# A spectral filter and an MLP on one core: the roots of tiles 0 and 1 move to ScalarE, the second fifth of W1 is loaded ahead of tiles 2 and 3

## The chip, the cores and the metric

The kernel runs on one core of a Trainium2 chip. The metric is device time in microseconds (us) of one execution; less is better. A core has five engines, each with its own instruction stream: TensorE (PE in the profile; its weight loads are shown apart as PEld), VectorE (DVE), ScalarE (ACT), GpSimd (POOL) and SyncE (SP), which here only issues DMA transfers. They work at the same time and wait for each other through semaphores. Matmul results land in PSUM, eight banks of which VectorE and ScalarE empty into SBUF.

## What is computed

```python
xn = _layernorm(x, axis=-1)                      # x: 2048 x 640, bf16
return x + _A_ref(xn, A_w_r, A_w_i) + _B_ref(xn, B_w1, B_b1, B_w2, B_b2)

def _layernorm(x, axis=-1, eps=1e-5):
    m = jnp.mean(x, axis=axis, keepdims=True)
    v = jnp.var(x, axis=axis, keepdims=True)
    return (x - m) / jnp.sqrt(v + eps)

def _A_ref(x, w_r, w_i):
    X = jnp.fft.rfft2(x.astype(jnp.float32), axes=(-2, -1)) * (w_r + 1j * w_i)
    return jnp.fft.irfft2(X, s=(S, D), axes=(-2, -1)).astype(jnp.bfloat16)

def _B_ref(x, w1, b1, w2, b2):
    h = _gelu(jnp.einsum("bsd,df->bsf", x, w1) + b1)     # w1: 640 x 1536
    return jnp.einsum("bsf,fd->bsd", h, w2) + b2         # w2: 1536 x 640
```

The layer norm has no learned scale. Its result goes through a two-dimensional Fourier filter and, apart from that, through a two-layer MLP with a gelu; both are added to x.

## The kernel before

The 2048 rows stand as 16 tiles of 128 partitions by 640 columns, x0 to x15. For each tile VectorE computes statistics of the two halves of the columns (L670), joins them to mean and variance (L672, tensor `mv`), and normalizes the tile into `T` with `(x - mean) * rstd` (L695). Between the two stands the reciprocal root `rstd`: GpSimd raises the variance (the epsilon is already in it) to the power -0.5 (L674). Tile 0 is normalized in two parts, columns 0 to 255 and 256 to 639, so that its first two blocks of 128 columns can go on early; all others in one.

A normalized tile is used twice. The MLP needs it transposed, in `xnT`: tiles 0 to 3 are transposed by TensorE against an identity matrix (L714) and copied out of PSUM by ScalarE (L561) or VectorE (L562); tiles 4 to 15 by a DMA transpose that SP issues (L702). The Fourier part folds each pair of tiles on VectorE (L726, L730), and TensorE multiplies the folds by the table `gtab` as the first step of the transform along the rows.

The first MLP layer contracts 640 columns in five blocks of 128, so W1 is loaded in five transfers of 128 x 1536, the fifths `w1_0` to `w1_4`. For tiles 0 and 1 the work is laid out by blocks: for each of the twelve 128-wide pieces of the hidden layer five matmuls add up in PSUM, those of fifths 0 and 1 for each tile apart (128 columns, "single-tile"), the rest for both tiles at once (256 columns). The gelu on ScalarE (L774) empties each result into `gT`. Then come tiles 2 and 3 and the later blocks, the Fourier steps in between, and the second layer, the inverse transform and the sum with x at the end.

What sets the order is a table written out by hand, `ORDER`: for each engine the numbers of all operations, in the order in which they stand on that engine. The numbers count the operations as the program creates them. A planner goes through the table with its own costs and landing times (`LAND`, `LATE`) to choose PSUM banks and buffers, and works out which operation has to wait for which; it doesn't change the order. So an engine that waits holds everything behind it. All matmuls but the transposes are recorded on L550, a helper's line.

The loads of x, W1 and the tables all go through SP's queue: x0, x1, w1_0, x2 and x3 in one transfer, w1_1, w1_2, w1_4, w1_3, x4 and x5, x6 and x7, gtab, and so on. `load_x(c, n)` loads n tiles from tile c in one transfer. ScalarE begins with a load of the table that holds the tanh gelu (L599); plain copies need no other table. Before the first real work TensorE runs 38 matmuls on zeros.

## Time and profile before

| what | us |
|---|---|
| median of three runs (146.36 to 146.63) | 146.58 |
| the profiled execution | 146.47 |
| its span, first to last instruction | 145.2 |
| TensorE busy | 139.2 |
| VectorE busy | 112.6 |
| ScalarE busy | 81.0 |
| GpSimd busy | 24.0 |

The profile is one execution. Each row of its timeline gives the start in us from the span's start, the duration of the group, the engine, the line, the operation, what it writes and reads, how many instructions are joined in the row, and in square brackets the idle time of that engine ahead of it and who ended it. A row with SPq is the issue of a transfer. A row of the list of DMA issues gives the size and the time from issue to landing; such rows are taken here over a window that holds one issue. The stretches give each engine's busy time within from:to, with the number of instructions, the granted TensorE clock, the DMA share and GB/s. The chain of work that ended last is listed in order of time as start, duration and what ran.

### The profile page before, as it was taken

The page shows a single profiled execution, that of the slowest core. Times are in us where ns is not written, and L with a number is a line of the kernel's source. Part 1 is how long each engine was busy: PE and PEld are TensorE (multiplying, and loading weights), DVE is VectorE, ACT ScalarE, POOL GpSimd, SP SyncE. Part 2 cuts the span into 40 slices and gives each one's busy share as a digit, 9 for nine tenths or more (in the row PEclk, how much of TensorE's full clock was granted, in tenths as well). Part 3 has the DMA queues.
Part 4 walks back from the last instruction along what each step waited for, and adds up shares of the span by engine and source line. Part 5 has one row for each costly group of instructions (what it writes and reads, how often), then busy time and mean ns, then how long its engine had stood idle before and what let it go on. Part 6 is the DMA issues. An engine that isn't in the chain of part 4 may idle for free.

```text
span 145.2 us, 4067 instructions
## 1 busy us (share of the span) xinstructions
PE 139.2 (96%) x1702; PEld 90.0 (62%) x1720; DVE 112.6 (78%) x235; ACT 81.0 (56%) x145; POOL 24.0 (17%) x40
## 2 busy tenths in 40 slices
PE   7799999999999999999999999999999999999994
PEld 7589998988465454446544645554446666656573
DVE  1999999999844449889966967992432998998984
ACT  3208999999989769763555633206376755201000
POOL 2330302206100027220100220000055700000000
DMA  4999998999997827939676571453559895103225
GB/s 109 337 403 347 319 172 265 155 181 235 268 188 151 192 51 147 228 86 179 130 202 123 62 151 34 41 120 80 95 108 212 178 214 183 58 5 135 93 103 168
DMA packets 30841, 23.63 MB, mean 163 GB/s; under 512 B 20456, under 2 KB 26856, under 8 KB 30696
## 3 DMA queue, kind: packets, MB, share of 16 engines
q1 hardware_dynamic: 28432, 17.81, 51.7%
q0 software_dynamic: 2368, 5.57, 17.9%
q8 instruction: 13, 0.21, 0.6%
q14 instruction: 4, 0.03, 0.1%
q10 hardware_dynamic: 24, 0.00, 0.0%
HBM read 13.54 MB, written 2.62 MB: 111 GB/s over the span
## 4 chain that ended last, share of the span: by engine, by line
PE 91%; DVE 4%; issue 2%; DMA 2%; POOL 0%
PE ps L550 91%; DVE stats L670 2%; DMA X<-in_A_x_dram 2%; DVE T L695 1%; DVE mv L672 0%; POOL rstd L674 0%; PE ps L714 0%; DVE xnT L562 0%; DVE W L957 0%
## 5 line engine op out<-in xcount | busy, mean ns | idle before, releaser
L550 PE MATMUL ps<-xnT,W 128*128 128x256 bf16 (+2 forms) x384 | 58.7, 300 | 0.1
L550 PE MATMUL ps<-W,gT 128*128 128x512 bf16 (+3 forms) x380 | 55.7, 292 | 1.6 <-issue 1.1
L550 PEld LDWEIGHTS ps<-W,gT 128*128 128x128 bf16 x396 | 30.3, 98 | 23.5 <-issue 1.6
L550 PEld LDWEIGHTS ps<-xnT,W 128*128 128x128 bf16 x384 | 33.3, 98 | 16.2 <-issue 1.6
L774 ACT ACTIVATE gT<-ps,b1col 128x256 bf16<-128x256 f32 (+1 forms) x72 | 35.3, 557 | 6.8 <-PE ps L550 6.5
L670 DVE BATCH_NORM_STATS2 stats<-X 128x6 f32<-128x320 bf16 x32 | 13.9, 475 | 2.1 <-DMA X<-in_A_x_dram 2.1
L561 ACT ACTIVATE Wf<-ps 128x960 bf16<-128x960 f32 (+1 forms) x8 | 7.0, 901 | 13.5 <-PE ps L550 13.5
L942 POOL DMA_DIRECT2D X<-in_A_x_dram x8 | 7.1, 1012 | 39.8 <-DMA Wf<-in_A_w_r_dram 17.0
L841 DVE TENSOR_TENSOR T<-Y,Wf 128x1288 bf16<-128x1288 bf16 x16 | 12.7, 825 | 0.0
L942 POOL DMA_DIRECT2D xnT<-in_A_x_dram x8 | 7.8, 1246 | 25.1 <-ACT xnT L924 25.1
L674 POOL TENSOR_TENSOR rstd<-mv,mhalf 128x2 f32<-128x2 f32 (+1 forms) x10 | 7.1, 714 | 26.6 <-DVE mv L672 26.5
L561 ACT ACTIVATE Xb<-ps 128x960 bf16<-128x960 f32 (+1 forms) x7 | 7.7, 1104 | 6.8 <-PE ps L550 6.7
L562 DVE CAST Y<-ps 128x644 bf16<-128x644 f32 x8 | 6.5, 828 | 5.4 <-PE ps L550 5.4
L561 ACT ACTIVATE XV<-ps 128x1280 bf16<-128x1280 f32 (+3 forms) x10 | 9.5, 962 | 0.7 <-PE ps L550 0.7
L562 DVE CAST Xb<-ps 128x960 bf16<-128x960 f32 (+1 forms) x5 | 5.9, 1177 | 4.1 <-PE ps L550 4.0
L730 DVE TENSOR_TENSOR T<-T 128x512 bf16<-128x512 bf16 (+1 forms) x32 | 8.5, 312 | 0.0
L695 DVE TENSOR_SCALAR T<-X,mv,rstd 128x640 bf16<-128x640 bf16 (+2 forms) x17 | 7.1, 430 | 0.9 <-POOL rstd L674 0.6
L896 DVE TENSOR_TENSOR Wf<-Wf 128x960 bf16<-128x960 bf16 (+1 forms) x12 | 7.0, 597 | 0.5 <-ACT Wf L561 0.3
L957 DVE TENSOR_TENSOR W<-ps,X 128x640 bf16<-128x640 f32 x8 | 6.5, 820 | 1.1 <-PE ps L550 1.1
L957 DVE TENSOR_TENSOR W<-ps,xnT 128x640 bf16<-128x640 f32 (+2 forms) x10 | 6.7, 686 | 0.7 <-PE ps L550 0.7
L845 DVE TENSOR_TENSOR Z<-T 128x644 bf16<-128x644 bf16 x16 | 7.1, 487 | 0.1
L550 PE MATMUL ps<-etab,XV 32*128 32x160 bf16 (+1 forms) x128 | 7.2, 232 | 0.0
(55 smaller groups left out, 130.5 us busy)
## 6 DMA issues: line engine op xcount, KB each, us to landing
X<-in_A_x_dram POOLq DMA_DIRECT2D x8, 320.0 KB, 4.6
xnT<-in_A_x_dram POOLq DMA_DIRECT2D x8, 320.0 KB, 5.0
out_dram<-W SPq DMA_DIRECT2D x15, 160.0 KB, 1.8
X<-in_A_x_dram SPq DMA_DIRECT2D x7, 320.0 KB, 7.3
W<-in_B_w_dram SPq DMA_DIRECT2D x5, 384.0 KB, 5.8
W<-in_B_w_dram SPq DMA_DIRECT2D x4, 480.0 KB, 7.6
Wf<-in_A_w_i_dram SPq DMA_DIRECT2D x6, 160.5 KB, 6.2
Wf<-in_A_w_r_dram SPq DMA_DIRECT2D x6, 160.5 KB, 3.9
```

Of the source, the lines that this page charges most:

```text
L550: ins = e.matmul(o_, lhsT=lw, rhs=rh, start=st, stop=sp_, skip_group_check=True)
L561: return e.activation(dst(), src(), ACT.Copy, scale=scale)
L562: return e.tensor_copy(dst(), src())
L670: st_op[c] = K.op([("dve", 0.393)], pr, lambda e, _, c=c, h=h: e.bn_stats(stats[:, c, 6 * h:6 * h + 6], view(X, c * D + H2 * h, [[1, H2]]) ...
L674: K.op([("pool", 0.65)], 500, lambda e, _, a=a, b=b: e.tensor_tensor(out=rstd[:, a:b], in0=mv[:, a:b, 1], in1=mhalf[:, a:b], op=ALU.pow), ...
L695: o = K.op([("dve", 0.066 + (d1 - d0) / 1980.0)], pr, lambda e, _, c=c, n=n, xnv=xnv, d0=d0, d1=d1: e.tensor_scalar(out=xnv(n, d0, [[1, d1 ...
L730: ring_ops.append(K.op([("dve", dve_us(4 * w, 2))], pr, lambda e, _, op=op, x1v=x1v, xfv=xfv, o_=o_, o0=o0, o1=o1, w=w: e.tensor_tensor(ou ...
L774: K.op([("act", act_us(128 * nt, 1))], pr + PRIO["gelu"] + GP[bi], lambda e, _, c0=c0, nt=nt, fc=fc, hps=hps, at=at: e.activation(gT[:, fc ...
L841: filt_ops.append(K.op([("dve", dve_us(4 * KP, 2))], pr, lambda e, _, k=k, Y=Y, TB=TB, pair=pair: e.tensor_tensor(out=view(TT, TB.slot * 8 ...
L845: K.op([("dve", dve_us(2 * KP, 2))], pr, lambda e, _, TB=TB, Z=Z, r=r, op=op: e.tensor_tensor(out=view(Zb, Z.slot * 4 * KP + r * KP, [[2 * ...
L942: xo_ops[c] = K.op([("pool", 0.9)], 51 - c / 20, lambda e, _, c=c, xov=xov: e.dma_start(xov(0, D), xv[:, c, :], accum_op=ALU.add), reads=[ ...
L957: K.op([("dve", dve_us(w))], 95, lambda e, _, os_=os_, fps=fps, o0=o0, w=w, xov=xov, base=base: e.tensor_tensor(out=view(W1, OST + os_.slo ...
```

## The change

Five things change, and with them the order table.

- The reciprocal roots of tiles 0 and 1 are no longer a power on GpSimd. ScalarE takes the square root of the variance, and VectorE the reciprocal of it, in place. All other tiles keep the power.
- ScalarE so loads two tables: the one with the square root first, and the one with the gelu later.
- Tile 1 is normalized in two parts, as tile 0 was.
- x2 and x3 are loaded in two transfers, and w1_1 stands ahead of both on SP.
- The numbers of `ORDER`, `LAND` and `LATE` are new.

```diff
 ORDER = {
-    "sp": """8 13 14 17 15 16 19 18 21 22 20 27 30 23 26 28 153 155 166 168 31 32 35 46 48 37 179 181 192 194 38 39 41 34 44 33
+    "sp": """8 14 15 16 18 19 17 21 20 23 24 22 29 32 25 28 30 158 160 171 173 33 34 37 48 50 39 184 186 197 199 40 41 43 36 46
...
-LAND = {8: 3.13, 13: 3.63, 14: 5.8, 15: 8.08, 16: 9.04, 18: 11.01, 19: 10.03, 20: 14.89, 21: 11.84, 22: 12.65, 23: 17.41, 26: 18.61, 27: 15.54, 28: 19.46, 30: 16.42}
+LAND = {8: 3.12, 14: 3.6, 15: 5.85, 16: 7.0, 17: 9.3, 18: 7.4, 19: 8.0, 20: 11.2, 21: 10.3, 22: 14.89, 23: 11.84, 24: 12.65, 25: 17.41, 28: 18.61, 29: 15.54, 30: 19.46, 32: 16.42}
...
-        K.op([("act", 1.3)], 420, lambda e, _: e.preload_act_table(ACT.Gelu_apprx_tanh), writes=[Buf("table")])
+        K.op([("act", 1.3)], 420, lambda e, _: e.preload_act_table(ACT.Sqrt), writes=[Buf("table")])
+        K.op([("act", 1.3)], 420, lambda e, _: e.preload_act_table(ACT.Gelu_apprx_tanh), writes=[Buf("table2")])
...
         load_w1(2)
-        load_x(2, 2)
+        load_x(2, 1)
+        load_x(3, 1)
         load_w1(3)
...
             a, b = c0, c0 + n
+            if a < 2:
+                B_sd = Buf(f"sd{a}")
+                K.op([("act", 0.1)], 500, lambda e, _, a=a: e.activation(rstd[:, a:a + 1], mv[:, a, 1:2], ACT.Sqrt), reads=[B_mv], writes=[B_sd])
+                K.op([("dve", 0.08)], 500, lambda e, _, a=a: e.reciprocal(rstd[:, a:a + 1], rstd[:, a:a + 1]), reads=[B_sd], writes=[B_rs[a]])
+                continue
             K.op([("pool", 0.65)], 500, lambda e, _, a=a, b=b: e.tensor_tensor(out=rstd[:, a:b], in0=mv[:, a:b, 1], in1=mhalf[:, a:b], op=ALU.pow),
...
-                cuts = (0, 256, D) if not c else (0, D)
+                cuts = (0, 256, D) if c < 2 else (0, D)
...
-                    if not c + j0:
-                        tp.deps.remove(norm_ops[1])
+                    if c < 2 and not j0:
+                        tp.deps.remove(norm_ops[2 * c + 1])
...
-                    free = norm_ops[:2 * ki + 3]
+                    free = norm_ops[:2 * ki + 4]
```

The last two hunks follow from the second part of tile 1: the first two blocks of a tile don't wait for its second part, and a list of normalizations has one entry more. Behind the first 40 us or so the order on TensorE is as it was, and on SP it differs only at the head.

Where the instructions stand is shown at three places. Lines in the changed kernel are a few higher or lower (L670 is L671, L695 is L701, L714 is L720, L550 is L549). SP, at its beginning, before:

```order
L545 DMA X<-in_A_x_dram 128x640 x2
L545 DMA W1<-in_B_w1_dram 128x1536
L545 DMA X<-in_A_x_dram 128x1280
L545 DMA W1<-in_B_w1_dram 128x1536 x4
L545 DMA X<-in_A_x_dram 128x1280 x2
```

and with the change:

```order
L544 DMA X<-in_A_x_dram 128x640 x2
L544 DMA W1<-in_B_w1_dram 128x1536 x2
L544 DMA X<-in_A_x_dram 128x640 x2
L544 DMA W1<-in_B_w1_dram 128x1536 x3
L544 DMA X<-in_A_x_dram 128x1280 x2
```

The second fifth has moved ahead of tiles 2 and 3, which are now two issues; the three other fifths follow as before, one issue later.

VectorE from the first statistics on (X is the loaded x, T the normalized tile and its folds, xnT the transposed tile), before:

```order
L670 BN_STATS stats<-X 128x6 x2
L672 BN_AGGR mv<-stats 128x2
L670 BN_STATS stats<-X 128x6 x2
L672 BN_AGGR mv<-stats 128x2
L695 TENSOR_SCALAR T<-X,mv,rstd 128x256
L695 TENSOR_SCALAR T<-X,mv,rstd 128x384
L695 TENSOR_SCALAR T<-X,mv,rstd 128x640
L562 COPY xnT<-ps 128x384
L670 BN_STATS stats<-X 128x6 x2
L562 COPY xnT<-ps 128x384
```

and with the change:

```order
L671 BN_STATS stats<-X 128x6 x3
L673 BN_AGGR mv<-stats 128x2
L671 BN_STATS stats<-X 128x6
L678 RECIPROCAL rstd<-rstd 128x1
L673 BN_AGGR mv<-stats 128x2
L701 TENSOR_SCALAR T<-X,mv,rstd 128x256
L701 TENSOR_SCALAR T<-X,mv,rstd 128x384
L678 RECIPROCAL rstd<-rstd 128x1
L701 TENSOR_SCALAR T<-X,mv,rstd 128x256
L701 TENSOR_SCALAR T<-X,mv,rstd 128x384
L732 TENSOR_TENSOR T<-T 128x2x320 x2
L561 COPY xnT<-ps 128x384 x2
```

Tile 0's mean and variance stand behind the first half of tile 1's statistics, each reciprocal behind the work that follows, and tile 0's and 1's folds ahead of the copies; the statistics of tiles 2 and 3 come behind both copies. Further down, tile 3's copy out of PSUM, which ScalarE had, stands on VectorE behind the first statistics of tile 4.

TensorE from the first transposes on (ident is the identity matrix, the 128x128 rows with W1 are the single-tile matmuls, the 128x256 rows those of both tiles; a wait on d_ is one for a transfer), before:

```order
L714 MATMUL ps<-ident,T 128x128 x3
L550 MATMUL ps<-xnT,W1 128x128 x2
L550 MATMUL ps<-xnT,W1 128x128 [waits s_act]
L550 MATMUL ps<-xnT,W1 128x128 x9
L550 MATMUL ps<-xnT,W1 128x128 [waits d_15]
L550 MATMUL ps<-xnT,W1 128x128 x17
L550 MATMUL ps<-xnT,W1 128x256 [waits d_16,s_dve]
L550 MATMUL ps<-xnT,W1 128x256 x7
L550 MATMUL ps<-xnT,W1 128x256 [waits d_19]
```

and with the change:

```order
L720 MATMUL ps<-ident,T 128x128 [waits s_dve]
L720 MATMUL ps<-ident,T 128x128 x2
L549 MATMUL ps<-xnT,W1 128x128 [waits d_16,s_act]
L549 MATMUL ps<-xnT,W1 128x128 x15
L549 MATMUL ps<-xnT,W1 128x128 [waits s_dve]
L549 MATMUL ps<-xnT,W1 128x128 x23
L549 MATMUL ps<-xnT,W1 128x256 [waits d_17,s_dve]
L549 MATMUL ps<-xnT,W1 128x256 x9
L549 MATMUL ps<-xnT,W1 128x256 [waits d_21]
```

d_15 before and d_16 with the change are the second fifth, d_16 before and d_17 now the third, d_19 before and d_21 now the fifth one. All 48 single-tile matmuls now stand ahead of the third fifth, where 40 stood, and ten two-tile matmuls behind it ahead of the next one, where eight stood. The two transposes of tile 1's first part stand ahead of the first W1 matmul, and the other three of tile 0 behind it.

21 lines of the change are left out of this document (10 added, 11 removed), and 36 rows, old and new, of the table ORDER.

## The prediction

> **What bounds the kernel now.** I read the page's totals first, then the busy time by stretches, the chain that ended last, and the timeline of the first 13 us.
>
> ```profile
> span 145.2 us, 4067 instructions
> PE 139.2 (96%) x1702; PEld 90.0 (62%) x1720; DVE 112.6 (78%) x235; ACT 81.0 (56%) x145; POOL 24.0 (17%) x40
> core 0: us, PE busy (x) PEld busy (x) DVE busy (x) ACT busy (x) POOL busy (x), PEclk, DMA share, GB/s
> 5.50:12.00 6.50, 6.35 (x83) 5.40 (x84) 6.24 (x20) 1.76 (x5) 1.66 (x4) 1.00 1.02 397
> 12.00:25.00 13.00, 13.00 (x139) 11.84 (x137) 12.75 (x42) 12.88 (x31) 2.12 (x3) 1.00 1.04 262
> 12.03 38.28 PE ps L550 x391
> 143.17 0.33 DVE W L957
> ```
>
> TensorE is busy 139.2 of 145.2 us, at the full granted clock (1.00). On the chain, one piece of TensorE work runs 38.28 us unbroken from 12.03, and after that only its own issue gaps part it, to 143.17. So a microsecond is to be had only before 12 us, and what is won there arrives at the end only if nobody holds TensorE later. The row from 12 to 25 us is the warning: there VectorE (12.75 of 13.00) and ScalarE (12.88) are as full as TensorE.
>
> Where TensorE waits early is seen in its weight loads, which run just ahead of the matmuls:
>
> ```profile
> 5.50 0.11 PEld L714 LDWEIGHTS ps<-ident,T 128*128 128x128 bf16 x2 [1.08 <-DVE T L695]
> 6.26 0.22 PEld L550 LDWEIGHTS ps<-xnT,W 128*128 128x128 bf16 x4 [0.27 <-ACT xnT L561]
> 7.07 1.75 PEld L550 LDWEIGHTS ps<-xnT,W 128*128 128x128 bf16 x30
> 9.03 1.02 PEld L550 LDWEIGHTS ps<-xnT,W 128*128 128x128 bf16 x10 [0.20 <-DVE T L695]
> 10.91 0.55 PEld L550 LDWEIGHTS ps<-xnT,W 128*128 128x128 bf16 x6 [0.15 <-DMA W<-in_B_w_dram]
> W<-in_B_w_dram SPq DMA_DIRECT2D x1, 384.0 KB, 5.8
> W<-in_B_w_dram SPq DMA_DIRECT2D x1, 384.0 KB, 6.3
> W<-in_B_w_dram SPq DMA_DIRECT2D x1, 384.0 KB, 6.8
> 2.67 1.93 SPq L545 DMA_DIRECT2D W<-in_B_w_dram  x4
> ```
>
> Real work starts at 5.50. The three waits after it are 0.27 (copy of tile 0's transpose), 0.20 and 0.15, together 0.62 us. The 0.20 is put down to a normalization that these matmuls don't read; they read the third fifth of W1. The four issues from 2.67 are 0.48 apart, so the third fifth, issued at 3.15, landed 5.8 later, at 8.95: that is the real releaser. The fifths issued at 3.63 and 4.11 landed at 9.9 and 10.9. Before 9.03 TensorE had run out of work on the first two fifths that its order allowed.
>
> **The roots.** Each of tiles 0 and 1 loses a POOL power and gains a ScalarE root and a VectorE reciprocal.
>
> ```profile
> 3.10 0.89 DVE L670 BATCH_NORM_STATS2 stats<-X 128x6 f32<-128x320 bf16 x2 [2.10 <-DMA X<-in_A_x_dram]
> 4.03 0.22 DVE L672 BATCH_NORM_AGGREGATE mv<-stats 128x2 f32<-128x15 f32 x1
> 4.17 0.82 DVE L670 BATCH_NORM_STATS2 stats<-X 128x6 f32<-128x320 bf16 x2
> 5.16 0.57 DVE L695 TENSOR_SCALAR T<-X,mv,rstd 128x256 bf16<-128x256 bf16 x2
> 5.92 0.45 DVE L695 TENSOR_SCALAR T<-X,mv,rstd 128x640 bf16<-128x640 bf16 x1 [0.19 <-POOL rstd L674]
> 4.33 0.58 POOL L674 TENSOR_TENSOR rstd<-mv,mhalf 128x1 f32<-128x1 f32 x1 [2.78 <-DVE mv L672]
> 1.45 1.28 ACT L599 ACT_TABLE_LOAD   x1 [1.45 <-PEq L985]
> 6.11 0.17 ACT L656 ACTIVATE b1col<-ps 128x12 f32<-128x12 f32 x1
> 10.64 0.70 ACT L561 ACTIVATE xnT<-ps 128x640 bf16<-128x640 bf16 x1 [3.44 <-PE ps L714]
> ```
>
> Tile 0's power ended at 4.33 + 0.58 = 4.91, yet its normalization started at 5.16, because VectorE was still at tile 1's statistics: POOL cost nothing there. The new chain has the same cover. The sum of tile 0 moves behind one piece of tile 1's statistics, to about 4.3, and ends at 4.5. No root or reciprocal stands in this trace. Below, the nearest small ACTIVATE is the 128x12 copy, 0.17; above, the power itself, 0.58. I take 0.17 for the root, since one element a row is nearest to twelve. A reciprocal I take at 0.14, the distance at which the next instruction followed the aggregate (4.03 to 4.17); bounds 0.1 to 0.3. So the root is there at 4.7, the reciprocal goes at 4.8 when VectorE comes free, and tile 0's first part starts at 5.1 to 5.2: 0.0, bounds -0.1 and +0.3. Tile 1 did wait for POOL, 0.19. It now starts near 5.75, and its first part (half of the 0.57 of two parts) ends at 6.05 where the whole ended at 6.37. TensorE's two transposes of it then fit into the 0.27 wait. But before, tile 0's other three stood there before 6.26, so the first W1 matmul still starts near 6.2 with one transpose more to do (0.06), which the 0.06 earlier start pays: 0.0.
>
> The second table load, 1.28 as the first, comes behind the copy of tile 1, about 6.8 to 8.1. The cover is the idle 3.44 that ScalarE had before 10.64; without it every gelu would start 1.28 later. Cost 0.0.
>
> **The second fifth first.** It goes to SP ahead of tiles 2 and 3.
>
> ```profile
> 1.73 0.43 SPq L545 DMA_DIRECT2D W<-in_B_w_dram  x1
> W<-in_B_w_dram SPq DMA_DIRECT2D x1, 384.0 KB, 4.1
> X<-in_A_x_dram SPq DMA_DIRECT2D x1, 320.0 KB, 4.4
> 2.20 0.43 SPq L545 DMA_DIRECT2D X<-in_A_x_dram  x1
> 0.81 0.88 SPq L545 DMA_DIRECT2D X<-in_A_x_dram  x2
> X<-in_A_x_dram SPq DMA_DIRECT2D x1, 160.0 KB, 2.3
> W<-in_B_w_dram SPq DMA_DIRECT2D x1, 384.0 KB, 4.9
> ```
>
> The first fifth landed at 1.73 + 4.1 = 5.83, tiles 2 and 3 at 2.20 + 4.4 = 6.6, the second at 2.67 + 4.9 = 7.57, and a fifth takes about 1.0 (8.95 to 9.9 to 10.9). So the second now lands near 6.8, in time for the point at which TensorE has used up the first (6.2 and eight matmuls and six transposes, 0.8: about 7.0). TensorE can then do all 48 single-tile matmuls ahead of the third fifth instead of 40. At 1.75/30 = 0.058 each (the row from 7.07), 8 more are 0.47: it reaches the third fifth at 8.82 + 0.47 = 9.29 instead of 8.82. The third fifth has the same bytes ahead of it as before, and one transfer more. Tiles 0 and 1, 160 KB each and issued 0.47 apart, both landed 2.3 after their issue, so two halves take at most 0.94 where the whole took 0.77: the third lands at 8.95 to 9.12. The wait of 0.20 goes. A two-tile matmul takes 0.10 to 0.11 (1.02 for ten in the row from 9.03, its last one cut short). Ten of them bring TensorE to 10.4 (next fifth needed, there at 9.9 to 10.1), six more and five transposes (0.66 + 0.29) to 11.3 (last fifth needed, there at 10.9 to 11.1). The wait of 0.15 goes too. Term: -0.35, bounds 0.0 and -0.40. SP has one issue more, 0.47, ahead of x4, gtab and the later loads; those queue behind 4 us of transfers, so it costs them the 0.0 to 0.17 of the split alone.
>
> The Trainium skill, "DMA: Bandwidth & Descriptors", section Bandwidth, speaks against the split: it asks for transfers of 1 MiB and gives 0.95 us for 64 KB and 6.15 us for 1 MB, an estimated 0.6 us fixed for each. By that the third fifth would land at 9.5 and the term be about -0.1 instead of -0.35. The 0.47 between tiles 0 and 1 contradicts 0.6 plus their bytes, so I keep the row.
>
> **What is late next.** Tiles 2 and 3 arrive about 0.6 to 1.0 later, and VectorE does more: two reciprocals, a part more (0.57 - 0.45 = 0.12), tile 0's folds ahead of its copies, and tile 3's copy, which was ScalarE's.
>
> ```profile
> 9.06 0.83 DVE L726 TENSOR_TENSOR T<-T 128x640 bf16<-128x640 bf16 x2
> 7.43 0.34 DVE L562 COPY xnT<-ps 128x384 bf16<-128x384 bf16 x1
> X<-in_A_x_dram SPq DMA_DIRECT2D x1, 320.0 KB, 7.1
> 4.64 1.14 SPq L545 DMA_DIRECT2D X<-in_A_x_dram  x2
> 16.05 0.43 DVE L695 TENSOR_SCALAR T<-X,mv,rstd 128x640 bf16<-128x640 bf16 x1
> 15.37 5.33 SPq L702 DMA_TRANSPOSE xnT<-T  x4
> xnT<-T SPq DMA_TRANSPOSE x1, 4.5
> 22.39 3.78 PE L550 MATMUL ps<-xnT,W 128*128 128x256 bf16 x33
> ```
>
> Tile 0's folds (0.83) now stand ahead of the copies of tiles 0 and 1, which so end near 7.5 and 7.8; the first matmul that reads one is the 25th single-tile one, sixteen behind the 7.0 above, at 7.9: 0.0, with 0.1 as bound. Tile 3's copy frees ScalarE of 0.70 in the full stretch and costs VectorE some 0.5 (0.34 for 384 columns). It stands behind tile 4's first statistics (tile 4 lands at 4.64 + 7.1 = 11.74, now up to 11.9), so ends near 12.8; TensorE wants it at 12.9. Cost 0.0, bounds 0.0 and 0.3. Further on, tile 5 was normalized at 16.05 and its transpose, the second of the four SP issues (from about 16.7), landed 4.5 later at 21.2; TensorE read it from 22.39, 1.2 later. If VectorE runs 0.8 late there (0.12 + 0.28 + 0.5, less some idle), it lands at 22.0, and TensorE, 0.35 earlier, wants it at 22.04. I take 0.05 for small waits in this stretch, bounds 0.0 and 0.6.
>
> Sum: 0.0 + 0.0 - 0.35 + 0.05 = -0.30. The profiled run took 146.47 (span 145.2 and 1.27 around it), so 146.17 against its own time; the median of the runs shown is 146.58, 0.11 above it, which gives 146.28.
>
> **Rivals.** (a) Won early, given back in the full stretch. ScalarE and VectorE have 0.12 and 0.25 us free of 13, and TensorE can't be ahead of their results. For it speaks that row, against it that ScalarE loses 0.70. With 0.3 given back: 146.6.
> (b) Slower by VectorE. If it is 1.5 late at tile 5, the transpose lands at 22.7 and TensorE stands 0.66 at its first matmuls on tiles 4 and 5; with the 0.35 won that is +0.31, or 146.9. The sign turns at 1.2 late. For it: 6.24 of 6.50 busy before and more work now; against it: I can count only 0.9.
> (c) The roots cost more. At 0.58 for a root, as the power, and 0.3 for a reciprocal, tile 0 starts some 0.3 late and tile 1 with it, which takes back what the fifths won: 146.6. Slower only if they start over 0.64 late, for which no row speaks.
> (d) The second fifth doesn't come earlier, because it was not the queue that held it. It lands at 7.5, TensorE waits 0.5 at 7.0: 0.5 - 0.35 = 0.15 slower, 146.7; with tiles 2 and 3 late as well, 146.9.
> (e) The split holds the queue up by a fixed time for each transfer. The wait for the third fifth returns from 0.34 on (9.29 - 8.95); at 0.6 it is 0.26, and 0.35 - 0.26 leaves 146.5. Against it stands the 0.47 between tiles 0 and 1. This is the rule of the skill that is named above.
>
> **Numbers.** A measurement of this kernel tells about 0.2% (0.29 us) from no change. Forecast (the early waits go and the later engines follow; 145.95 to 146.45): 0.50, of it 0.36 below 146.29 and 0.14 within. (a) 0.19: 0.03 faster, 0.13 within, 0.03 slower. (b) 0.16, slower. (c) 0.06: 0.04 within, 0.02 slower. (d) 0.05: 0.01 within, 0.04 slower. (e) 0.04, within. Faster 0.39, same 0.36, slower 0.25. The range takes in (a) to (e) and most of the far bounds of the terms: 145.8 to 147.1.
>
> **What would show it.** Right: no wait in the weight loads before the first double matmuls and before the last fifth; the second fifth landing before 7.0; both roots under 0.25 and the second table load inside ScalarE's idle time; TensorE unbroken from about 11.3. Wrong: a wait of TensorE on tile 3's copy near 12.9, or on the transpose of tile 5 near 22 (b), or on gelus between 13 and 35 (a); a first transpose past 5.6 (c); a wait on the second fifth near 7 (d).

## The result, and the profile after

The changed kernel takes 148.49 us (median, 148.44 to 148.67) against 146.61 for the kernel before beside it: 1.0122 times as long, 95% interval 1.0091 to 1.0153. The forecast was 146.28, in a range of 145.8 to 147.1. Sign and range are both wrong. Ratios are taken over the executions that the chip's slower state left alone, so a ratio need not be the quotient of the two medians.

The profiled execution took 148.67, with a span of 147.1. So 1.57 us lie around the span, where 1.27 lay before: of the 2.20 between the two profiled executions, 1.9 are in the span and 0.3 outside it. The page, first the span and the busy times, then two of its costliest groups:

```profile
span 147.1 us, 4092 instructions
PE 141.6 (96%) x1720; PEld 90.1 (61%) x1720; DVE 113.3 (77%) x239; ACT 82.2 (56%) x147; POOL 23.0 (16%) x38
L549 PE MATMUL ps<-xnT,W 128*128 128x256 bf16 (+2 forms) x384 | 59.2, 300 | 1.5 <-DVE xnT L561 1.3
L671 DVE BATCH_NORM_STATS2 stats<-X 128x6 f32<-128x320 bf16 x32 | 14.0, 476 | 3.6 <-DMA X<-in_A_x_dram 3.6
```

TensorE's first-layer matmuls now have a wait of 1.3 for a copy that VectorE makes (`xnT`), and VectorE's statistics wait for loads of x. The same two stretches as before:

```profile
5.50:12.00 6.50, 6.08 (x85) 5.39 (x86) 5.93 (x21) 2.57 (x5) 1.61 (x2) 1.00 0.99 356
12.00:25.00 13.00, 11.70 (x124) 10.20 (x123) 11.53 (x36) 11.45 (x28) 1.45 (x2) 1.00 0.83 222
```

From 12 to 25 us TensorE, VectorE and ScalarE were all full; now all three have lost 1.2 to 1.4 of the 13 at the same time. The chain that ended last names where:

```profile
5.05 8.68 DMA X<-in_A_x_dram
13.73 0.02 issue
13.76 0.49 DVE stats L671
14.25 0.40 DVE xnT L561
14.65 0.05 issue
14.70 11.83 PE ps L549 x121
26.53 0.08 issue
26.61 118.39 PE ps L549 x1462
145.00 0.02 issue
145.03 0.32 DVE W L963
```

The load of tile 4, issued at 5.05, takes 8.68; VectorE's first statistics of it wait for that, tile 3's copy stands behind them, and TensorE behind the copy. Before, the chain had TensorE unbroken from 12.03, and VectorE's last instruction at 143.17. The timeline shows the parts of the change one by one:

```profile
4.60 0.20 ACT L677 ACTIVATE rstd<-mv 128x1 f32<-128x1 f32 x1 [1.85 <-DVE mv L673]
4.83 0.16 DVE L678 RECIPROCAL rstd<-rstd 128x1 f32<-128x1 f32 x1
5.43 0.11 PEld L720 LDWEIGHTS ps<-ident,T 128*128 128x128 bf16 x2 [0.66 <-DVE T L701]
6.90 1.28 ACT L599 ACT_TABLE_LOAD   x1
7.03 2.27 PEld L549 LDWEIGHTS ps<-xnT,W 128*128 128x128 bf16 x40
9.52 1.44 PEld L549 LDWEIGHTS ps<-xnT,W 128*128 128x128 bf16 x14 [0.21 <-issue]
11.84 0.28 PEld L720 LDWEIGHTS ps<-ident,T 128*128 128x128 bf16 x5 [0.17 <-DVE T L701]
13.76 0.49 DVE L671 BATCH_NORM_STATS2 stats<-X 128x6 f32<-128x320 bf16 x1 [1.44 <-DMA X<-in_A_x_dram]
14.16 0.47 DVE L561 COPY xnT<-ps 128x640 bf16<-128x640 bf16 x1
14.69 1.31 PEld L549 LDWEIGHTS ps<-xnT,W 128*128 128x128 bf16 x13 [1.58 <-DVE xnT L561]
```

And the issues of the second fifth (2.20), the third (3.62) and tile 4 (5.05), each from a window of its own; the last number is the time to landing:

```profile
W<-in_B_w_dram SPq DMA_DIRECT2D x1, 384.0 KB, 4.4
W<-in_B_w_dram SPq DMA_DIRECT2D x1, 384.0 KB, 5.8
X<-in_A_x_dram SPq DMA_DIRECT2D x1, 320.0 KB, 8.7
```

So the second fifth landed at 6.6, the third at 9.4 (8.95 before), tile 4 at 13.7 (11.7 before). A transfer is spread over sixteen DMA engines. The packets in the trace show that fifteen parts of tile 4 landed between 11.30 and 12.15, and one at 13.73. In the same stretch the trace has one packet of a queue that no load uses. The queues from 11 to 12 us:

```profile
q1 hardware_dynamic: 169, 0.41, 101.6%
q8 instruction: 1, 0.02, 6.2%
```

6.2% of sixteen engines for 1 us is one engine for all of it. The packet has 16,384 bytes, began at 11.65 and took 0.99. There are 13 of them over the execution (12.78 was the first before). The first question was whether this packet, the split or the copy's place made the loss.

### The profile page after: what moved, and what is told of

Its sections match the earlier page's. It is cut to its first block, busy times and chain, and to the rows that moved or that the text cites. A ratio compares the mean times of both kernels' runs of the same rounds, so it can differ in the third digit from the quotient of the medians.

```text
span 147.1 us, 4092 instructions
## 1 busy us (share of the span) xinstructions
PE 141.6 (96%) x1720; PEld 90.1 (61%) x1720; DVE 113.3 (77%) x239; ACT 82.2 (56%) x147; POOL 23.0 (16%) x38
## 4 chain that ended last, share of the span: by engine, by line
PE 89%; DMA 6%; SPq 3%; DVE 1%; issue 0%
PE ps L549 89%; DMA X<-in_A_x_dram 6%; SPq L544 3%; DVE stats L671 0%; DVE xnT L561 0%; DVE W L963 0%
## 5 line engine op out<-in xcount | busy, mean ns | idle before, releaser
L549 PE MATMUL ps<-xnT,W 128*128 128x256 bf16 (+2 forms) x384 | 59.2, 300 | 1.5 <-DVE xnT L561 1.3
L549 PE MATMUL ps<-W,gT 128*128 128x512 bf16 (+3 forms) x396 | 58.7, 295 | 0.0
L549 PEld LDWEIGHTS ps<-W,gT 128*128 128x128 bf16 x396 | 30.3, 98 | 23.5 <-issue 1.6
L549 PEld LDWEIGHTS ps<-xnT,W 128*128 128x128 bf16 x384 | 33.1, 98 | 17.3 <-issue 1.8
L671 DVE BATCH_NORM_STATS2 stats<-X 128x6 f32<-128x320 bf16 x32 | 14.0, 476 | 3.6 <-DMA X<-in_A_x_dram 3.6
L680 POOL TENSOR_TENSOR rstd<-mv,mhalf 128x2 f32<-128x2 f32 (+1 forms) x8 | 6.2, 779 | 29.1 <-DVE mv L673 29.1
L701 DVE TENSOR_SCALAR T<-X,mv,rstd 128x640 bf16<-128x640 bf16 (+2 forms) x18 | 7.1, 410 | 1.1 <-POOL rstd L680 1.1
L732 DVE TENSOR_TENSOR T<-T 128x640 bf16<-128x640 bf16 x16 | 7.3, 474 | 0.1
```

Of the source, the lines that this page charges most:

```text
L549: ins = e.matmul(o_, lhsT=lw, rhs=rh, start=st, stop=sp_, skip_group_check=True)
L671: st_op[c] = K.op([("dve", 0.393)], pr, lambda e, _, c=c, h=h: e.bn_stats(stats[:, c, 6 * h:6 * h + 6], view(X, c * D + H2 * h, [[1, H2]]) ...
L701: o = K.op([("dve", 0.066 + (d1 - d0) / 1980.0)], pr, lambda e, _, c=c, n=n, xnv=xnv, d0=d0, d1=d1: e.tensor_scalar(out=xnv(n, d0, [[1, d1 ...
L732: K.op([("dve", dve_us(640, 2))], pr, lambda e, _, k=k, op=op, xnv=xnv, x1v=x1v: e.tensor_tensor(out=x1v(H2 * k, [[D, 2], [1, H2]]), in0=x ...
```

## The experiments

All ratios are to the kernel before, run beside each on the same chip, with 95% intervals; 0.1% is 0.15 us. The changed kernel stands at 1.0122 (1.0091 to 1.0153) in four executions and at 1.0074 (1.0029 to 1.0118) in ten later ones. The interval of every variant of it below overlaps both, so no variant's time by itself shows that something came back. Orders are shown as diffs of the operations on one engine; "the order of before" and "the later order" are those of the kernel before and of the changed kernel.

### Does the split cost a fixed time?

The kernel before with x2 and x3 in two transfers:

```diff
-        load_x(2, 2)
+        load_x(2, 1)
+        load_x(3, 1)
```

> The kernel before with x2 and x3 in two transfers where the one stood; the second fifth stays behind them. Theory (one transfer more costs the queue 0.5 to 0.6, as the changed kernel with one transfer for both showed: third fifth at 8.78 against 9.41): second fifth at 8.0 to 8.2 instead of 7.54, third at 9.4 to 9.5 instead of 8.92, tile 4 near 12.2, or near 13.5 if the instruction packet of 12.8 still meets it; TensorE waits about 0.4 for the second and 0.5 or more for the third fifth, of which the later order gives some back: 0.3 to 0.6 % over before. Rival (the split costs 0.0 to 0.17 as forecast, and the later third fifth came from the order or the second table load): third at 8.9 to 9.1, time within 0.1 % of before.

Measured: 1.0041 (1.0021 to 1.0062); ten executions between 147.04 and 147.83. In its profile the two halves landed only 0.42 apart (6.33 and 6.75). The second fifth landed at 9.2, later than expected because a few single packets took up to 1.16, the third at 10.2, and TensorE waited:

```profile
9.25 2.07 PEld L553 LDWEIGHTS ps<-xnT,W 128*128 128x128 bf16 x28 [1.03 <-DMA W<-in_B_w_dram]
```

The time, 0.6 us over before and clear of the noise, puts the rival (0.0 to 0.17 for the split) out. This wait does not show why: two profiles with one transfer for both tiles have the like when single packets are slow (0.89 with both tables loaded, 0.62 with the unused reciprocals). The converse, the changed kernel with one transfer for both:

```diff
-        load_x(2, 1)
-        load_x(3, 1)
+        load_x(2, 2)
```

> The changed kernel with x2 and x3 in one transfer again, behind the second fifth. Theory (the split costs about 0.46, the distance at which the third fifth landed later than before, 9.41 against 8.92): the third fifth lands at 8.9 to 9.0, TensorE's wait of 0.21 for it goes; tile 4's first fifteen sixteenths land at 11.7, and the last one near 13.5, since the instruction packet still meets it; time 148.0 to 148.3. Rival 1 (the loads are slower at 6 to 8 us for another reason, the second table load or the order of rows): the third fifth still lands at 9.3 to 9.4, time 148.4 to 148.6. Rival 2 (0.4 earlier is enough for tile 4 to pass the packet): tile 4 at 11.8, time 146.8 to 147.2.

Measured: the third fifth, now issued at 3.15, landed 5.6 later, at 8.8, so the split had cost it 0.6 in this pair of profiles (9.4 against 8.8). Over all profiles the third fifth landed at a median of 9.5 in nine with the split and 8.9 in eleven without, each with a scatter of up to 0.7. The time, 1.0111 (1.0074 to 1.0148), doesn't show it, for another reason:

```profile
6.33 0.64 PEld L553 LDWEIGHTS ps<-xnT,W 128*128 128x128 bf16 x6
7.78 4.66 PEld L553 LDWEIGHTS ps<-xnT,W 128*128 128x128 bf16 x54
```

The six weight loads that took 0.37 in the changed kernel (6.25 there) take 0.64. TensorE ran at half pace up to 9.8, so it came 1.5 late to tile 2's transposes, and the instruction packet with it (12.89): tile 4 landed at 11.6, the packet met gtab. Nothing about the full loss follows from this run.

The kernel before with the second fifth ahead of the unsplit tiles 2 and 3:

```diff
 SP
+DMA w1_1
 DMA x2, x3
-DMA w1_1
```

> The kernel before with one move on SP: the second fifth of W1 ahead of x2 and x3, which stay one transfer; no other engine's order is touched. Theory 1 (the third fifth and tiles 2 and 3 set the early stretch, not the second fifth): the second fifth lands at 6.6 to 6.9, tiles 2 and 3 at 7.5 to 8.0, the third fifth as before near 8.9, so TensorE's wait for it stays at 0.2; tile 2's transposes (10.06 before) come 0.0 to 0.4 later since its normalization is later: 0.0 to 0.3 % over before. Theory 2 (as forecast, the second fifth held TensorE up): 0.1 to 0.2 % below before.

Measured: 1.0028 (0.9995 to 1.0060), six of ten executions at 146.4 to 146.9, others up to 148.2. No gain, as theory 1 had it. But its profile is not the one that theory 1 foretold: the second fifth landed at 7.9, not at 6.6 to 6.9, and tiles 2 and 3 only at 8.7. VectorE stood for them, and TensorE for a copy of tile 1 that VectorE makes behind their statistics:

```profile
8.74 0.89 DVE L673 BATCH_NORM_STATS2 stats<-X 128x6 f32<-128x320 bf16 x2 [2.10 <-DMA X<-in_A_x_dram]
9.93 0.99 PEld L553 LDWEIGHTS ps<-xnT,W 128*128 128x128 bf16 x10 [0.95 <-DVE xnT L565]
```

So this run tells what the move costs in the order of before, not what an early second fifth is worth.

### Do the roots cost anything?

The kernel before with the roots alone:

```diff
-  preload(gelu)
+  preload(Sqrt) ... preload(gelu) behind tile 1's copy
-  POOL  rstd = var ** -0.5                  (tiles 0, 1)
+  ACT   rstd = sqrt(var);  DVE  rstd = 1 / rstd
```

> The kernel before with only the roots changed: square root on ScalarE, reciprocal on VectorE for tiles 0 and 1, the square root's table first and the gelu's behind tile 1's copy; tile 1 still in one part. Theory (the 0.33 outside the span comes with the root or the reciprocal themselves, since loading both tables without using the root left it at 1.27, and the span is not touched): 1.57 to 1.66 between span and time, span as before within 0.15, time 0.2 % over before. Rival (the 0.33 comes with the changed order): 1.27, time within 0.1 % of before.

Measured: 1.0070 (1.0047 to 1.0094), 1.61 to 1.67 between span and time, but also a TensorE wait of 1.02 at 15.36 for a gelu. The planner, given the roots' own costs, had chosen other PSUM banks behind them. Told costs that keep every bank, the same change gives:

```diff
-  planner's cost of root, reciprocal: 0.1, 0.08
+  planner's cost of root, reciprocal: 0.5, 0.05
```

> The kernel before with only the roots changed as in the run of the roots alone, but with the planner told costs that leave all PSUM banks as before. Theory (the roots cost nothing inside the span; the 1.0 wait for a gelu near 15.4 came from the other banks): no wait near 15, span as before within 0.15, 1.57 to 1.66 between span and time: 0.1 to 0.35 % over before. Rival (ScalarE's second table load or the reciprocals delay the work at 12 to 16 us): a wait of 0.5 or more there again, 0.5 to 0.8 % over before.

Measured: 0.9990 (0.9958 to 1.0023), spans 145.0 to 146.1, and 1.59 to 1.67 outside. Its page and the end of its chain:

```profile
span 145.2 us, 4088 instructions
...
143.16 0.32 DVE W L966
```

VectorE's last instruction starts at 143.16, against 143.17 before: the roots and the second table load cost nothing inside the span. The 0.33 outside is theirs, and three runs look for it. Both tables, no root:

```diff
-  preload(gelu)
+  preload(Sqrt) ... preload(gelu) behind tile 1's copy
```

> The kernel before with only ScalarE's table loads changed: the square root's table first, the gelu's behind the copy of tile 1; nobody uses the root. What it is to settle: the runs of the changed kernel lie 1.57 to 1.66 above their spans, those of the kernel before 1.27 to 1.3, so 0.33 of the loss lies outside the span. Theory A (that 0.33 belongs to ending on, or starting with, another table set): time 0.3 above before, at an unchanged span. Theory B (it belongs to something else, for instance the number or order of instructions): time as before within 0.15. If the second table load also slows the loads at 7 to 8 us, the third fifth of W1 lands at 9.2 or later instead of 8.9, and the span grows by 0.2 to 0.4; if it doesn't, the third fifth stays at 8.9 to 9.0.

Measured: 1.0011 (0.9984 to 1.0038); 1.22 to 1.31 outside. Both tables again, and two square roots that nobody reads:

```diff
+  ACT   spare = sqrt(var)                   (tiles 0, 1; unused)
```

> The kernel before with both tables loaded and two square roots on ScalarE whose results nobody reads; the powers on GpSimd stay, there is no reciprocal. If the use of the square root brings the time outside the span: 1.57 to 1.66 between span and time, 146.9 to 147.2. If it is the reciprocal: 1.22 to 1.31, 146.6 to 146.9.

Measured: 0.9981 (0.9940 to 1.0022); 1.22 to 1.31. Two reciprocals that nobody reads:

```diff
+  DVE   spare = 1 / rstd                    (tiles 0, 1; unused)
```

> The kernel before with two reciprocals of a 128x1 column added on VectorE behind tile 0's and tile 1's normalization; nobody reads their results, and the powers on GpSimd and the one table load stay. If VectorE's reciprocal brings the time outside the span: 1.57 to 1.67 between span and time. If it came with the missing powers on GpSimd: 1.22 to 1.31. Inside the span 0.0 to 0.3 more, since VectorE has 0.3 more to do.

Measured: 0.9993 (0.9965 to 1.0020); 1.22 to 1.31. So neither tables nor root nor reciprocal brings it alone. What is common to all runs with 1.56 to 1.69 is that GpSimd lacks two powers; that, or root and reciprocal together, is left, and wasn't separated. (The run with 58 warm-up matmuls, below, scatters from 1.27 to 2.19 outside the span, and it has the powers.) The changed kernel with the powers back:

```diff
-  ACT   rstd = sqrt(var);  DVE  rstd = 1 / rstd
+  POOL  rstd = var ** -0.5                  (tiles 0, 1; one table)
```

> The changed kernel with the roots of tiles 0 and 1 as powers on GpSimd again and one table load, all else as changed (tile 1 still in two parts). Theory (the roots neither win nor lose inside the span; the loss there is the late tile 4 and the copy behind it): the first transposes start at 5.4 to 5.5, tile 4 lands at 13.5 to 13.8, TensorE waits 1.3 to 1.6 near 13.4, span within 0.2 of the changed kernel's 147.1; the 0.33 outside the span goes if it belongs to the tables: 1.0 % over before. Rival (the roots or the second table load are what costs): the third fifth lands below 9.0 and tile 4 below 12.5, time within 0.3 % of before.

Measured: 1.0063 (1.0030 to 1.0096), 1.22 to 1.32 outside. Inside the span it was not as expected: tile 4 landed at 12.3, and tile 6 was the late one (14.1), with a VectorE wait of 0.9 for it.

### The copy of tile 3

The kernel before with only that copy moved:

```diff
 ACT
 gelu
-copy xnT3
 DVE
 statistics of x4, first half
+copy xnT3
```

> The kernel before with one move: tile 3's copy out of PSUM goes from ScalarE to VectorE, behind tile 4's first statistics, as in the changed kernel. As forecast (tile 4 lands at 11.7, the copy ends near 12.7, just when TensorE wants it): 0.0 to 0.3 us over before, no wait of over 0.3 near 13. Theory now (the place is only as good as tile 4's landing, which was on time before because the instruction packet came at 12.8, behind it; and VectorE has no time to give): a TensorE wait of 0.0 to 0.3 near 13 and some 0.3 to 0.5 given up between 16 and 27 us: 0.1 to 0.4 % over before. A wait of over 1 near 13 would say that the copy's place alone does it, without the packet.

Measured: 1.0041 (1.0020 to 1.0062). Tile 4 landed on time (11.7), and yet the copy started at 12.94, because VectorE came to tile 4 only at 12.54:

```profile
12.54 0.49 DVE L672 BATCH_NORM_STATS2 stats<-X 128x6 f32<-128x320 bf16 x1
12.94 0.48 DVE L564 COPY xnT<-ps 128x640 bf16<-128x640 bf16 x1
```

```profile
13.60 1.98 PEld L552 LDWEIGHTS ps<-xnT,W 128*128 128x128 bf16 x19 [0.62 <-DVE xnT L564]
```

The place alone costs 0.62 here, without a late load. In the changed kernel, the copy ahead of the statistics:

```diff
 DVE
+copy xnT3
 statistics of x4, first half
-copy xnT3
```

> The changed kernel with one move on VectorE: tile 3's copy out of PSUM stands ahead of tile 4's first statistics. Theory (the loss is TensorE's wait of 1.3 to 1.6 for that copy, which VectorE holds behind tile 4's late landing): the copy runs at 12.3 to 12.8, TensorE meets no wait near 13.4, and 1.3 to 1.5 come back: 147.0 to 147.2, though tile 4 still lands at 13.7. Rival 1 (tile 4 is late for everything that reads it, and the full stretch from 12 to 25 us takes the gain back): 148.1 to 148.5. Rival 2 (the loss lies in the later order, where the offset grows by another 0.3 to 0.5 up to 44 us): the wait near 13 goes, and the time falls by less than 1.0.

Measured: 1.0065 (1.0032 to 1.0098). The wait at 13 is gone, and the time stayed above the 147.0 to 147.2 of the theory (median 147.91). TensorE waited 0.87 for the second fifth at 7 us, the sign of rival (d): it landed at 7.8 here. VectorE still waits for a load, now of tile 6 (which landed at 14.7):

```profile
12.89 0.49 DVE L565 COPY xnT<-ps 128x640 bf16<-128x640 bf16 x1
13.30 0.48 DVE L675 BATCH_NORM_STATS2 stats<-X 128x6 f32<-128x320 bf16 x1
14.76 0.49 DVE L675 BATCH_NORM_STATS2 stats<-X 128x6 f32<-128x320 bf16 x1 [0.97 <-DMA X<-in_A_x_dram]
```

And the copy back on ScalarE:

```diff
 DVE
-copy xnT3
 ACT
 gelu
+copy xnT3
```

> The changed kernel with tile 3's copy back on ScalarE, where the kernel before had it (behind the first gelu); all else as changed. Theory (the copy is what ties TensorE to tile 4's landing, and VectorE is too full to take it): TensorE has no wait of over 0.3 near 13 even if tile 4 lands at 13.7, VectorE starts tile 4's other statistics 0.47 earlier, and the time falls by 1.0 to 1.4 against the changed kernel: 0.2 to 0.5 % over before, of which 0.2 is outside the span. Rival (tile 4's own lateness costs the same a little later, at the first Fourier steps near 20 us or at the gelus near 26 us): 0.8 to 1.2 % over before.

Measured: 1.0098 (1.0062 to 1.0133), the time of the rival. No wait at 13 but 0.21, tile 4 at 12.2, tile 6 at 14.0; VectorE waited 1.26 for tile 6, and TensorE in small pieces that the profile puts to gelus:

```profile
14.00 1.28 DVE L675 BATCH_NORM_STATS2 stats<-X 128x6 f32<-128x320 bf16 x3 [1.26 <-DMA X<-in_A_x_dram]
```

```profile
PEld ps L553 <- ACT gT L784: 1.3, 4, 0.5
```

(The second fence is the first row of a list of who TensorE's weight loads waited for from 12 to 44 us: total, times, longest. Before, that list has one row, 0.3, for VectorE. What the two larger of these four waits were is read below, at the second profile of the changed kernel.)

### The instruction packet

The changed kernel with fewer, wider warm-up matmuls:

```diff
-WARM = (38, 0)          # 38 matmuls of 128 columns
+WARM = (10, 0)          # 10 matmuls of 512 columns
```

> The changed kernel with the warm-up on zeros written as 10 matmuls of 512 columns instead of 38 of 128 (the same work in time, 28 matmuls and 28 weight loads fewer). Theory (one DMA engine was held by a 16 KB packet of the instruction queue at 11.65, 0.99 long, when TensorE had issued a certain number of instructions, and so one sixteenth of tile 4 came 1.6 behind the other fifteen): with 56 instructions fewer the packet comes some 28 matmuls later, near 14.5; tile 4 lands at 12.2, the copy of tile 3 ends near 13.2, and the time is 147.0 to 147.4; gtab or x6 carries the delay instead. Rival (tile 4 is late through the queue: split, row sizes or the table load): tile 4 lands at 13.7 as before, and the time stays at 148.3 to 148.6.

Measured, in the profile: the packet at 14.13, tile 4 at 12.25, tile 6 at 13.07, and neither VectorE nor TensorE with a wait there:

```profile
12.28 0.49 DVE L675 BATCH_NORM_STATS2 stats<-X 128x6 f32<-128x320 bf16 x1
12.69 0.47 DVE L565 COPY xnT<-ps 128x640 bf16<-128x640 bf16 x1
13.10 1.67 DVE L675 BATCH_NORM_STATS2 stats<-X 128x6 f32<-128x320 bf16 x4
...
61.36 0.82 DVE L958 TENSOR_TENSOR X<-ps,X 128x640 f32<-128x640 f32 x1 [1.46 <-PE ps L553]
```

The packet follows TensorE's instructions, and with it gone from there tile 4 was on time. But the time did not fall: 1.0113 (1.0068 to 1.0157). The last row shows one place where that profile lost again: VectorE waits 1.46 for a tile that is loaded a second time there, and TensorE about 1.0 behind it. I took it for the work of a later packet, which began at 57.9 and took 1.83: fifteen parts of that reload landed by 59.5, one at 61.3. The unused reciprocals, in the order of before, bear this out. They have the same wait (1.50 at 61.35) with a packet at 58.7, fifteen parts by 59.4 and one at 61.3. So this loss belongs to no order: it depends on what a packet meets. Moved by 44 instructions instead of 56:

```diff
-WARM = (38, 0)          # 38 matmuls of 128 columns
+WARM = (16, 0)          # 16 matmuls of 306 columns
```

> The changed kernel with the warm-up on zeros as 16 matmuls of 306 columns instead of 38 of 128, 44 instructions fewer. Theory (the first instruction packet comes some 2 later, 13.3 to 13.8, behind tiles 4 and 6; VectorE has no wait of over 0.3 between 12.5 and 16.5, TensorE none of over 0.5 between 12 and 27; what stays is 0.33 outside the span and 0.4 to 0.8 of waits at 25 to 36 us of the later order): 0.4 to 0.8 % over before, against 1.2 % of the changed kernel. Rival (the waits come back elsewhere in full): 1.0 % or more over before, with a wait of TensorE of over 0.7 that is not at a reload of x.

Measured: 1.0063 (1.0031 to 1.0096), as expected in time; 1.57 to 1.69 outside the span. The packet came at 14.7, later than the 13.3 to 13.8 expected, behind tiles 4 and 6. TensorE was at half pace to 10.0 in this profile, so it came to the same instruction later, and it lost another 1.0 at the reload near 62. The other way round, the kernel before with more instructions ahead:

```diff
-WARM = (38, 0)          # 38 matmuls of 128 columns
+WARM = (58, 0)          # 58 matmuls of 80 columns
```

> The kernel before with the warm-up written as 58 matmuls of 80 columns instead of 38 of 128, so with 40 instructions more ahead of the real work. Theory (the packet of the instruction queue follows TensorE's count of instructions): it comes 20 matmuls earlier, near 10.7 instead of 12.78, and one sixteenth of tiles 4 and 5 or of the last fifth of W1 lands about 1 later (tile 4 at 12.5 to 13.2 instead of 11.7), gtab about 1 earlier relative to it. Tile 3's copy is ScalarE's there and waits for no load, so TensorE has no wait of over 0.3 near 13 if the last fifth is not the one that is met: 146.5 to 147.0; if the last fifth is met, up to 147.8. Rival (the packet's time is chance, or set by something else): the packet near 12.8, tile 4 at 11.7, time 146.4 to 146.7.

Measured: the packet came at 10.94, and tile 6 landed at 13.47 instead of 12.54, tile 4 on time: so it was tile 6 that it met. The time, 1.0040 (0.9998 to 1.0083), scatters from 146.5 to 149.5 and decides nothing.

The changed kernel once more:

> The changed kernel once more, unchanged. Theory (the instruction packet comes at 11.4 to 12.2 in every execution and holds up one sixteenth of tile 4 or of tile 6, whichever of the two it meets): one of the two lands 1.0 to 1.6 late, at 13.5 to 14.8, VectorE idles 0.9 to 1.5 between 12.5 and 16.5, and the times lie between 147.9 and 148.9. Rival (the profile of the changed kernel was an odd one out): both land by 13.2, VectorE without a wait there, and most times below 147.6.

Measured: median 148.42 of ten (147.13 to 149.35) beside 146.72; ratio 1.0074 (1.0029 to 1.0118). The packet came at 11.52 and met tile 6 (issued at 5.9, 13.6 instead of 13.1), not tile 4, and VectorE waited only 0.41. TensorE lost its time later. VectorE's row, and the first row of the list from 12 to 44 us:

```profile
13.64 1.67 DVE L671 BATCH_NORM_STATS2 stats<-X 128x6 f32<-128x320 bf16 x4 [0.41 <-DMA X<-in_A_x_dram]
```

```profile
PEld ps L549 <- ACT gT L780: 1.1, 3, 0.7
```

The list names ScalarE's gelus. But the profile infers who released a wait, and the two larger of these three ended with something else, a transpose made by DMA. (From tile 4 on the normalized tiles are turned by DMA, one transfer for each, issued by SP.) The larger wait, and the issue of tile 7's transpose at 21.20:

```profile
25.68 0.35 PEld L549 LDWEIGHTS ps<-xnT,W 128*128 128x128 bf16 x4 [0.75 <-ACT gT L780]
```

```profile
xnT<-T SPq DMA_TRANSPOSE x1, 4.4
```

This matmul is the first that reads tiles 6 and 7. The gelu that had to free its PSUM bank ended at 24.94; tile 7's transpose landed at 25.62, and TensorE went on 0.06 later. The wait of 0.21 at 34.82 ended 0.06 after tile 11's transpose landed (34.76). Together they come to the 1.0 by which this span (146.2) exceeds that of before (145.2).

All waits of over 0.2 between 23 and 36 us that the profiles of the later order put to gelus end so, 0.05 to 0.06 after the landing of tile 5's, 7's or 11's transpose. The 0.33 at 26.58 in the first profile is one of them.

The next instruction packet has a part in it. It came at 23.42 here, between the landings of tiles 6 and 7. In ten of the twenty profiles it began while the transposes of tiles 4 to 7 were under way. Tile 7's then took 3.8 to 4.5 from issue to landing, against 2.7 to 3.1 in the other ten. In the first profile it began at 24.25: fifteen parts of tile 7's transpose landed by 24.80, one at 26.52. No run moves this packet alone.

So the 1.5 at 14 us of the first profile is one form of the loss, not all of it.

### Is it the waits, or is there too much in the order?

VectorE made tolerant of both loads:

```diff
 DVE
 fold of x2, x3, first half
+copy xnT3
+fold of x2, x3, second half
 statistics of x4, first half
-copy xnT3
-statistics of x6, first half
 statistics of x5, x5, x4
+statistics of x6, first half
```

> The changed kernel with VectorE's order alone rearranged at one place: behind the first fold of tiles 2 and 3 come tile 3's copy and the second fold, which read no late transfer, and only then tile 4's statistics; tile 6's first statistics stand behind tiles 4 and 5's, not in second place. Theory (VectorE's wait for tile 4 or 6 is the loss): VectorE's idle time between 12.5 and 16.5 falls from 1.44 to 0.0 to 0.5, TensorE's waits between 12 and 27 add up to less than 0.6 instead of 1.8, and 0.9 to 1.4 come back: 0.3 to 0.7 % over before. Rival (VectorE simply has too much to do): idle time falls, but TensorE waits as much in all between 16 and 36 us, 0.9 to 1.3 % over before.

Measured: 1.0126 (1.0045 to 1.0208) in four executions, the time of the rival. VectorE had no wait for a load from 12.5 to 16.5, and TensorE lost its time later:

```profile
23.62 2.42 PEld L553 LDWEIGHTS ps<-xnT,W 128*128 128x128 bf16 x23 [1.14 <-ACT gT L784]
```

Again it isn't the gelu, which had ended at 21.95. This is the first matmul on tiles 4 and 5. Fifteen parts of tile 5's transpose landed by 21.29, one at 23.56, and the second packet began at 21.84. So the rival's reason, that VectorE has too much to do, is not shown. Nor is the order alone changed: the planner gave 60 of 135 PSUM buffers other banks, and a wait of 1.49 for a gelu at 52.62 is 0.31 in the changed kernel.

At last, three parts of the change taken back together:

```diff
-  ACT   rstd = sqrt(var);  DVE  rstd = 1 / rstd
+  POOL  rstd = var ** -0.5                  (tiles 0, 1; one table)
-  load_x(2, 1); load_x(3, 1)
+  load_x(2, 2)
 DVE
+copy xnT3
 statistics of x4, first half
-copy xnT3
```

> The changed kernel with three of its parts taken back: roots on GpSimd with one table load, x2 and x3 in one transfer (behind the second fifth), and tile 3's copy ahead of tile 4's statistics. What is left is the second fifth ahead of tiles 2 and 3, tile 1 in two parts and the later order. Theory (those three carry the whole loss: 0.33 outside the span, the copy's wait 1.3 to 1.5, the split 0.2): third fifth at 8.8 to 9.0, no wait of TensorE of over 0.2 between 7 and 20 us, 1.27 around the span, time 0.1 to 0.4 below before. Rival 1 (the later order on VectorE and ScalarE from 20 to 44 us loses 0.4 by itself): 0.1 to 0.4 above before. Rival 2 (TensorE, earlier, meets another late transfer, since the instruction packet only falls on the next one): a new wait of 0.5 to 1.0, 0.3 to 0.6 % above before.

Measured: 1.0060 (1.0023 to 1.0097), or 0.9 us. That is more than the 0.1 to 0.4 of rival 1. It is the size of rival 2, with a new wait of 0.5, but the packet is not what did it: it met gtab. 1.24 to 1.31 lie outside the span, and VectorE waits for no load. The two largest rows of TensorE's waits from 12 to 44 us:

```profile
PEld ps L716 <- DVE T L697: 0.5, 1, 0.5
PEld ps L552 <- ACT gT L776: 0.4, 2, 0.3
```

The 0.5 is tile 3's normalization, late since tiles 2 and 3 landed at 8.0. Of the 0.4, 0.26 ended with tile 11's transpose (landed 34.35). Neither row stands in the list of before. The two, 0.8, are what this span (146.0) has over that of before. No run here is faster than the kernel before by more than the intervals.

## Why the prediction was wrong

**What bounds the kernel** held: the early waits were the only place to win, and the row from 12 to 25 us was the warning. It was weighed too lightly (rivals (a) and (b), 0.19 and 0.16).

**The roots** held inside the span (0.0 forecast; 145.2 with the roots alone, 145.2 before). Root 0.20 (0.17 forecast), reciprocal 0.16 (0.14), first transposes at 5.43. The 0.33 outside the span was in no term: my sum moved only the span and took what lies around it as fixed.

**The second table load** held: 6.90 to 8.18, inside ScalarE's idle time.

**The second fifth first** failed by its size: -0.35 forecast, about -0.1 measured. The fifth landed at 6.6 (6.8 forecast), and TensorE did its 48 single-tile matmuls ahead of the third. But the third landed at 9.4, not at 8.95 to 9.12, so the wait of 0.20 stayed at 0.21; the last fifth's 0.15 went, and a wait of 0.17 for tile 3's normalization (11.84) came. Counted over all matmuls up to 12.5 us, TensorE had lost 0.1 less than before. The mis-sized term is the split, 0.0 to 0.17 forecast, 0.6 measured (9.4 against 8.8, and 0.6 of time in the order of before). I had taken the distance of two transfers at the head of an empty queue (0.47) as its price. The Trainium skill, "DMA: Bandwidth & Descriptors", section Bandwidth, was nearer: the estimate of 0.6 fixed for a transfer, worked out from that page, agrees with these runs in size, and its -0.1 for the term too. That the 0.6 is a fixed time for each transfer is not shown: in the run of the split alone the two halves landed 0.42 apart, and slow single packets had a part in the delay. Rival (e) had this part right, with a chance of 0.04.

**What is late next** is the step that failed in sign: tile 3's copy, forecast at 0.0 with bounds 0.0 and 0.3. By its place alone it costs 0.62, and in the changed kernel's first profile 1.58 of weight-load wait. Two errors are in it. VectorE reaches tile 4's statistics by its own work only at 12.2 to 12.5, so a copy behind them ends at 13.1 to 13.4, not at 12.8. And tile 4's landing was taken from one row, 11.74, with the split's delay of at most 0.17 added; it was 13.73, since that row held only as long as nothing else fell on one of the sixteen engines. That tile 4 was met is chance in part: it happened in one of the ten profiles with the later order, and in the changed kernel's other profile tile 4 landed at 12.3 and tile 6 was the late one. The prediction named the sign to look for, a wait on the copy near 12.9, and gave it no rival of its own.

**Beyond that step** the loss isn't one wait. Between 23 and 36 us TensorE stood for DMA transposes of tiles that VectorE had normalized, in nine of the ten profiles with the later order (0.2 to 1.1 in all) and in none of the ten with the order of before. That is the mechanism of rival (b), a transpose that lands late, at tiles 7 and 11 where it named tile 5. Three things come together. The transposes land later: tile 11's landed at 34.1 to 35.9, where the order of before has 32.3 to 34.4. VectorE has more to do (113.3 busy against 112.6) in a stretch without slack, and it waits for loads; the two were not separated. Tile 7's is late when an instruction packet meets it. And the later order has no room: TensorE reads tile 11 at most 1.0 after the landing, against 1.9 to 3.3. Three profiles with the order of before had such a packet at tile 6 or 7 too, and TensorE came 0.3 to 1.2 after the landing.

The list of waits for gelus that rival (a) named as its sign does appear, but in these ten profiles TensorE waited for a gelu itself at most 0.3 at a time up to 44 us. In two it also stood 0.5 and 0.7 for a fold of VectorE near 20. The changed kernel differs from before in the PSUM banks of 51 buffers too. That was not tested by itself; the waits above end with landings, whatever the bank.

The parts can't be added up. By itself, in the order of before, the split costs 0.6, the copy's place 0.6, the move of the roots 0.33, all of it outside the span, and the earlier fifth nothing that the interval shows. With the first three undone 0.9 is still left. The loss itself was measured as 1.0122 and as 1.0074, and its form differs from one execution to the next with what the packets meet. What makes the 0.33 outside the span stays open.

## What to carry to other kernels

Before an instruction is moved onto an engine that is full, ask when that engine itself gets there, not when the data does; and don't queue work that the bottleneck needs behind a wait for a load. A landing time from one trace is the time of the slowest of sixteen parts, and it can move by 1 to 2 us when the order of something unrelated moves. Where a profile names who ended a wait, compare the end of that work with the end of the wait, and look for a landing between them. Compare the time around the span as well as the span.

## What the runs showed of the hardware that was not expected

- TensorE's instructions come in over the same DMA engines as the loads: 13 packets of 16 KB, each holding one engine for 0.9 to 1.9 us (14 with 58 warm-up matmuls). They follow the instruction count: 56 instructions fewer moved the first from 11.65 to 14.13, 40 more from 12.78 to 10.94. One part of the transfer in flight landed 1.6 to 1.8 later than the other fifteen (tile 4 at 13.73 against 12.15, tile 7's transpose at 26.52 against 24.80, a reload of x at 61.25 against 59.41).
- Splitting one transfer of 320 KB in two went with the next weight transfer landing 0.6 later in a busy queue (median 9.5 against 8.9), though the halves themselves landed as little as 0.42 apart.
- TensorE's pace after the idle start changed at different times under the same code: a warm-up matmul of 128 columns took 107 ns up to 3.7 us before, up to 4.5 in the changed kernel's first profile and to the end of the warm-up (4.9) in its second. With one transfer for tiles 2 and 3 the half pace lasted to 9.8, though the profile's granted clock reads 1.00 throughout. The Trainium skill, "TensorE: Matmul & The Clock Gate", Part 1, tells of a change from half to full rate after about 4 us of work, at a point in a free-running window of 3.4 us; the traces agree in the two rates (107 ns, then 56), but not in the time: the change came 2.6 us after TensorE's start before, 3.4 in the changed kernel's first profile, and at 9.8 in the run with one transfer.
- 0.33 us outside the span came with moving two powers off GpSimd, and with none of the added operations alone. Both together were not tried without that move.
- The planner's costs are part of a kernel: the same order with other costs got other PSUM banks, and a wait of 1.0.
